# Second layer of a three-stage kernel: block products summed in PSUM, multiplications on VectorE, plain products for two weight sets, waves of 8, 8 and 2 token tiles

## The chip, the core and the metric

The kernel runs on one core of a Trainium2 chip. The metric is the device time of one execution in microseconds (us). The engines are TensorE (PE for its matmuls, PEld for its weight loads), VectorE (DVE), ScalarE (ACT), GpSimd (POOL) and SyncE (SP, which issues the DMAs). All matrix products accumulate in PSUM, which has 8 banks of 128 x 512 float32.

## What is computed

```python
scores = scale * np.matmul(q, k.transpose(0, 1, 3, 2)) + bias      # attention, 4 x 8 heads, 576 tokens, depth 64
x = softmax(scores) @ v                                            # as 2304 tokens x 512
h = x @ w_in;  x = (h - np.tanh(h)) @ w_out                        # first layer, 512 -> 2048 -> 512
g = x @ w_gate                                                     # second layer, 512 -> 1536
silu = g * (1.0 / (1.0 + np.exp(-g)))
val = x @ w_val
return (silu * val @ w_out).astype(np.float32)                     # 1536 -> 512
```

Everything is float32. The change concerns the last four lines, and the hand-over from the first layer to them.

## The kernel before

**Products in three passes.** Each operand is split into a high part (the value rounded to the format that PE multiplies) and a low part (the rest). `matmul3` (L716) forms a product from three matmuls: high x high, high x low, low x high. A split costs one copy on ACT and one subtraction on DVE or POOL; all subtractions go through the helper `subtract` (L62).

**Second layer in quads.** For a pair of 128 x 2 output features ("weight set", 12 of them, gate and value in turn) and 768 of the 2304 tokens (three groups p), the 2 x 2 block product is a quad n, 36 in all: n // 3 is the weight set, n % 3 the token group. A quad is formed by the Strassen-Winograd scheme: seven products P1 to P7 (`PRODUCTS`, L927) of 6 matmuls of 384 columns each, in place of eight. The price are sums and differences: of weights (`combine_w`), of activations (`combine_x`, operands T1 to T4, from the accumulators acc of the first layer), and of results (`add`, `copy_one`). Three PSUM banks serve a quad (`QUAD_BANKS`): bank 0 for P1 and P2, bank 1 for P6, P7 and P4, bank 2 for P5 and P3. P1 is copied to SBUF as s1 by ACT, and DVE adds s1 to what stands in bank 1 after P6, then after P7, then after P4, so each of these products waits for DVE to have read the one before it.

**Pointwise part.** For a gate quad ACT takes the sigmoid, then block 0 is multiplied on DVE (`times_one`) and the other three blocks at once on POOL (`times_rest`, L1173, 1152 columns). For a value quad the same multiplications take the stored gate result, and the product goes to DRAM (`store`).

**Order of work.** The program order of each engine is its order on the chip. `begin` (L1184) interleaves the first quad with the last two output products of the first layer (tiles y). `step(n)` (L1206) handles the first products of quad n and the last ones of quad n - 1. Weights are read as raw 64-bit values and decoded ahead (`decode_first`, `decode_second`) on ACT, DVE and POOL, at places in the steps that `plan_decode` fixes.

**Output product.** `finish` (L1282) goes through the tokens in three waves of six tiles of 128 tokens. For each of the 12 feature chunks of a wave it loads 768 tokens back (DMA), splits them (`stage`: copy on ACT, subtraction on DVE) and runs 6 x 3 matmuls of 512 columns (tiles o). Results leave through three row buffers (`rows`).

## Time and profile before

| | |
|---|---|
| median of 3 runs | 1176.49 us (1172.83 to 1177.21) |
| profiled execution, its own time | 1175.12 us |
| its span, first to last instruction | 1173.3 us |
| PE busy | 1114.2 us, 95%, 7736 matmuls |
| DVE busy | 913.2 us, 78% |
| ACT busy | 742.0 us, 63% |
| POOL busy | 602.4 us, 51% |

Attention takes the first 294 us, the first layer runs to about 711 us, the second layer begins at 698.8 us between the first layer's last products, and the output product begins at 1009.4 us. A busy PE is not PE at its peak: matmuls are pipelined, so start-to-start distances are read instead of durations. Times in the rows below are in us from the start of the span, but "mean ns" in ns. In a timeline row the columns are start, duration, engine, line, operation, output tile <- input tiles, shape, number of merged instructions, and in brackets the idle time of the engine before the row with what ended it.

### The profile page before, as it was taken

Reading aid. Unit: us, or ns where it says so; the run is one execution under the profiler, and the core shown is the slowest. Engines: PE = TensorE matmul, PEld = TensorE weight load, DVE = VectorE, ACT = ScalarE, POOL = GpSimd, SP = SyncE. Lnnn points to the kernel's source line nnn. Section 1 sums busy time; section 2 is a strip of 40 time slices with the busy share of each in tenths; the row PEclk is TensorE's granted clock in tenths of the full one; section 3 lists DMA queues with packets and bytes.
Section 4 is the critical chain, followed back from the end, with each engine's and each line's share of the span. In section 5 each row is a group of like instructions: output and inputs, shape, how many; then the busy total and the mean of one; then the engine's idle time right before and its main releaser. Section 6 shows DMA issues by size and latency. Waiting matters only on the chain.

```text
span 1173.3 us, 21360 instructions
## 1 busy us (share of the span) xinstructions
PE 1114.2 (95%) x7736; PEld 924.1 (79%) x7736; DVE 913.2 (78%) x1732; ACT 742.0 (63%) x1463; POOL 602.4 (51%) x553
## 2 busy tenths in 40 slices
PE   8999999999999999999999996789999999899998
PEld 4577777777688888888888775788999899778886
DVE  7878999999699899889888899777777876873222
ACT  7989999998688887778778774333334334252222
POOL 3367777776363544355254445665666566660000
PEclk9999999999999999999999998899999999999999
DMA  5863535351112012011101100132231421554342
GB/s 193 278 191 89 146 95 156 88 164 40 37 55 72 19 54 60 13 55 55 36 19 36 36 1 1 36 126 89 91 107 48 152 90 67 189 182 159 94 158 85
DMA packets 92745, 107.46 MB, mean 92 GB/s; under 512 B 45280, under 2 KB 70112, under 8 KB 92640
## 3 DMA queue, kind: packets, MB, share of 16 engines
q1 hardware_dynamic: 92640, 106.10, 28.7%
q8 instruction: 61, 1.00, 0.4%
q14 instruction: 44, 0.36, 0.1%
HBM read 75.41 MB, written 30.67 MB: 90 GB/s over the span
## 4 chain that ended last, share of the span: by engine, by line
PE 69%; DVE 15%; ACT 5%; POOL 5%; issue 4%; DMA 2%; SPq 0%; POOLq 0%; DVEq 0%; ACTq 0%
PE h L720 14%; PE y L720 14%; PE b L720 12%; PE o L720 10%; PE x L436 7%; PE s L315 6%; DVE w L62 2%; PE pTa L381 2%; DVE bits_gate L1044 1%; DVE bits_gate L1035 1%; DVE bits_out L1044 1%; DMA bias<-bev 1%; PE pTb L381 1%; POOL bits_out L1037 1%; DVE acc L879 1%
## 5 line engine op out<-in xcount | busy, mean ns | idle before, releaser
L720 PE MATMUL y<-gh,w 128*128 128x512 f32 (+1 forms) x748 | 197.8, 369 | 3.2 <-POOL gh L62 1.5
L720 PE MATMUL h<-xh,w 128*128 128x512 f32 (+1 forms) x640 | 191.1, 369 | 0.0
L720 PEld LDWEIGHTS y<-gh,w 128*128 128x128 f32 x748 | 133.8, 188 | 28.9 <-POOL gh L62 2.5
L359 POOL TENSOR_SCALAR p<-p,r 128x576 f32<-128x576 f32 x144 | 109.2, 769 | 50.3 <-PE s L315 14.3
L720 PEld LDWEIGHTS h<-xh,w 128*128 128x128 f32 x640 | 116.9, 189 | 20.7 <-issue 0.5
L720 PE MATMUL h<-xl,w 128*128 128x512 f32 (+1 forms) x320 | 117.9, 368 | 0.0
L341 ACT ACTIVATE p<-p,m 128x576 f32<-128x576 f32 x144 | 111.1, 775 | 1.2 <-DVE m L330 0.8
L330 DVE CUSTOM_DVE_ANT_0 p<-s,bt 128x576 f32<-128x576 f32 x144 | 103.7, 753 | 10.5 <-PE s L315 10.3
L720 PE MATMUL o<-w,xh 128*128 128x512 f32 x324 | 100.0, 390 | 0.0
L826 ACT ACTIVATE sq<-h 128x512 f32<-128x512 f32 (+1 forms) x80 | 44.3, 554 | 64.2 <-PE h L720 64.2
L720 PE MATMUL b<-xh,w 128*128 128x384 f32 x288 | 81.0, 338 | 1.1 <-ACT s L1145 1.1
L720 PE MATMUL y<-gl,w 128*128 128x512 f32 (+1 forms) x212 | 78.9, 372 | 2.3 <-POOL gl L62 2.3
L720 PE MATMUL b<-xh,acc2r 128*128 128x384 f32 x288 | 80.5, 337 | 0.0
L315 PEld LDWEIGHTS s<-k,q 64*128 64x128 f32 x768 | 57.5, 184 | 28.4 <-issue 17.6
L436 PE MATMUL x<-pt,vn 128*64 128x256 f32 (+1 forms) x512 | 79.1, 421 | 0.2 <-DVE xl L451 0.2
L837 DVE TENSOR_TENSOR t<-h,sq 128x512 f32<-128x512 f32 (+1 forms) x80 | 51.4, 643 | 32.6 <-ACT th L827 32.2
L62 POOL TENSOR_TENSOR gl<-g,gh 128x512 fp32r<-128x512 f32 (+1 forms) x27 | 33.2, 1229 | 84.6 <-issue 42.1
L1173 POOL TENSOR_TENSOR sq<-sq,g 128x1152 f32<-128x1152 f32 x18 | 50.4, 2800 | 45.9 <-ACT g L1168 45.9
L315 PE MATMUL s<-k,q 64*128 64x288 f32 x768 | 72.9, 310 | 0.1
L720 PEld LDWEIGHTS o<-w,xh 128*128 128x128 f32 x324 | 61.1, 189 | 12.4
L1173 POOL TENSOR_TENSOR sq<-v,sq 128x1152 f32<-128x1152 f32 x18 | 53.1, 2948 | 31.4 <-DVE v L1150 31.4
L720 PE MATMUL o<-w,xl 128*128 128x512 f32 x162 | 63.5, 392 | 5.3 <-DVE xl L62 5.3
(209 smaller groups left out, 3099.9 us busy)
## 6 DMA issues: line engine op xcount, KB each, us to landing
raw_out<-in_moe_w_out_dram SPq DMA_DIRECT2D x28, 512.0 KB, 3.5
s<-sq SPq DMA_DIRECT2D x36, 384.0 KB, 2.6
bias<-bev SPq DMA_DIRECT2D x36, 320.0 KB, 3.5
bt<-bias SPq DMA_DIRECT2D x16, 576.0 KB, 4.9
xh<-s SPq DMA_DIRECT2D x24, 384.0 KB, 3.6
raw_in<-in_moe_w_in_dram SPq DMA_DIRECT2D x16, 512.0 KB, 3.8
raw_gate<-in_moe_w_gate_dram SPq DMA_DIRECT2D x12, 512.0 KB, 5.0
raw_val<-in_moe_w_val_dram SPq DMA_DIRECT2D x12, 512.0 KB, 3.6
```

The lines of the kernel that those rows point to most:

```text
L62: (engine or nc.gpsimd).tensor_tensor(out, a, b, ALU.subtract)
L315: nc.tensor.matmul(self.st[u][j][:, e, 0:HALF], lhs, k[r, y, e * HALF:(e + 1) * HALF], start=n == 0, stop=n == 2,)
L330: nc.vector.tensor_tensor_reduce(out=p[:, n, :].rearrange("p (e f) -> p e f", e=2), in0=ps[n][:, :, 0:HALF], in1=bt[:, n, :].rearrange("p ...
L341: nc.scalar.activation(p[:, n, :], p[:, n, :], AF.Exp, bias=m[:, n:n + 1], scale=-1.0, accum_out=ls[:, n:n + 1],)
L359: nc.gpsimd.tensor_scalar(p[:, n, :], p[:, n, :], r[:, n:n + 1], 1.0, ALU.mult, ALU.mult)
L381: nc.tensor.transpose(half[h][:, 64 * m:64 * m + 64], p[r, j, k:k + 128], self.ident[r, r])
L436: nc.tensor.matmul(ps[r, 0:n], lhs, rhs, start=c == 0, stop=c == 4)
L720: nc.tensor.matmul(out, lhs[a], rhs[b], start=first and n == 0, stop=last and n == 2, skip_group_check=again)
L826: nc.scalar.activation(u, h, AF.Square)
L837: nc.vector.tensor_tensor(t, h, u, ALU.mult)
L1044: nc.vector.scalar_tensor_tensor(w, q["m"], MIN_HIGH * MIN_HIGH, w, ALU.is_ge, ALU.mult)
L1173: self.nc.gpsimd.tensor_tensor(to, self.rest(n), q["g"] if n // 3 % 2 == 0 else to, ALU.mult)
```

## The change

- **Sums in PSUM.** ACT copies P1 from bank 0 into bank 1 of the same quad (`copy_one`), and P6, P7 and P4 accumulate on that copy. ACT copies bank 1 to SBUF after P6 (u2) and P5 to SBUF (p5); DVE adds p5 to bank 1 after P7, and u2 to bank 2 after P3. P2 moves from step n to step n + 1.
- **Multiplications on DVE.** Blocks 0 and 2 are multiplied on DVE straight from PSUM (`point_one`), blocks 1 and 3 together from SBUF (`times_pair`, 768 columns). POOL keeps the sums of decoding and of `combine_w`.
- **Plain products.** The quads 0 to 5 (`PLAIN`, the first two weight sets) use no scheme: four blocks of 12 matmuls each, in four banks in turn, each multiplied from its bank as soon as it stands. Their weight sets need no sums, and the activations only the splits of the four blocks. The differences T1 to T4 are formed later (`later`, `flush_later`), between the blocks of the quads 0 to 5.
- **Waves.** The output product runs in waves of 8, 8 and 2 token tiles; a stage is 1024 tokens of one chunk, and in the last wave 256 tokens of four chunks. Three loads are in flight, nine row buffers stand ready, and the last tile leaves in two halves, copied by DVE and ACT. Stage 0 is loaded and split one step earlier.
- Buffers are moved to make room (`kept`, the accumulators in halves, other slots); decoding has other places in the steps.

```diff
+        self.kept = ctx.enter_context(self.tc.tile_pool(name="b_kept", bufs=1)).tile([128, 3, 512], F32, name="kept")
...
+PLAIN = 6
+SET_SLOTS = ((16, 17, 18, 19, 27, 28, 29), (20, 21, 22, 23, 24, 25, 26))
...
+PLAIN_BANKS = ("h2", "h0", "h1", "h3")
...
+BLOCKS = ((0, 0), (1, 0), (0, 1), (1, 1))
+WAVES = ((0, 8), (8, 8), (16, 2))
+LAST_C = 4
...
+        mixed = V if p == 2 else G
+        self.queue += [
+            high("B11", b11), high("B21", b21), low("B11", b11), low("B21", b21, mixed),
+            high("B12", b12), high("B22", b22), low("B12", b12), low("B22", b22, mixed),
+        ]
+        one = [high("T1", b11), low("T1", b11)]
+        three = [high("T3", b12, 2), low("T3", b12)]
+        self.later += [((1, 1, 2)[p], f) for f in (
+            sub(b11, b12, b11), sub(b12, b22, b12), sub(b22, b22, b11), high("T2", b22, 0), sub(b21, b21, b22),
+            low("T2", b22), high("T4", b21, 4), low("T4", b21), *(() if p else three),
         )]
-        self.queue += [(t2, f) for f in (high("T2", b22, 0), low(V, "T2", b22))]
-        self.queue += [(t3, f) for f in (high("T3", b12, 2), low(G, "T3", b12))]
-        self.queue += [(t4, f) for f in (high("T4", b21, 4), low(V, "T4", b21))]
-    def flush(self, n, now):
-        while n and (f := next((f for f in self.queue if f[0] <= now), None)):
-            self.queue.remove(f)
-            f[1]()
+        self.later += [(p + 4, f) for f in one]
+        if p:
+            self.later += [(p + 3, f) for f in three]
+        self.later.sort(key=lambda f: f[0])
...
+            if plain:
+                self.sets[s] = dict(
+                    A11=(h1[:, L], l1[:, L]), A12=(h1[:, R], l1[:, R]), A21=(h2[:, L], l2[:, L]), A22=(h2[:, R], l2[:, R]),
+                )
...
+            when = ((n - 6, 1), (n - 5, 0), (n - 5, 1), (n - 4, 0), (n - 3, 0), (n - 3, 1), (n - 3, 1), (n - 2, 0))
+            for at, f in sorted(zip(EARLY.get(s, when), work), key=lambda e: e[0]):
+                add(*at, *f)
...
+            add(n + 2, 0, self.split_out, c)
             add(n + 1, 1, self.decode_second, q)
-            add(n + 2, 2, self.split_out, c)
-            add(n, 2, self.decode_first, q)
+            add(n + 1, 0, self.decode_first, q)
...
-        first = k in ("P1", "P5", "P6")
+        first = k in ("P1", "P5")
...
     def copy_one(self, n):
+        banks = self.quads[n]["banks"]
+        if banks[1] is None:
+            banks[1] = self.bank(QUAD_BANKS[n % 2][1], f"b1_{n}")
+        self.nc.scalar.copy(banks[1][:, 0:U2], banks[0][:, 0:U2])
...
+    def copy_two(self, n):
         q = self.quads[n]
-        q["s1"] = self.shared.tile([128, U2], F32, tag=f"one{n % 2}", name=f"s1_{n}")
-        self.nc.scalar.copy(q["s1"], q["banks"][0][:, 0:U2])
-    def add(self, n, to, bank, b=None):
+        q["u2"] = self.shared.tile([128, U2], F32, tag=f"one{n % 2}", name=f"u2_{n}")
+        self.nc.scalar.copy(q["u2"], q["banks"][1][:, 0:U2])
...
+        out = self.sq[n % 3][:, 1 + 2 * i] if self.is_gate(n) else self.pair(n)[:, i]
+        self.nc.vector.tensor_tensor(out, q["banks"][bank][:, 0:U2], q[b], ALU.add)
+    def point_one(self, n, at, src):
+        to = self.sq[n % 3][:, at]
+        if self.is_gate(n):
+            g = self.pair(n)[:, 2]
+            self.nc.scalar.activation(g, src, AF.Sigmoid)
+            self.nc.vector.tensor_tensor(to, src, g, ALU.mult)
+        else:
+            self.nc.vector.tensor_tensor(to, src, to, ALU.mult)
+    def sigmoid_pair(self, n):
+        if self.is_gate(n):
+            self.nc.scalar.activation(self.pair(n)[:, 0:2], self.sq[n % 3][:, 1::2], AF.Sigmoid)
+    def times_pair(self, n):
+        to = self.sq[n % 3][:, 1::2]
+        self.nc.vector.tensor_tensor(to, to, self.pair(n)[:, 0:2], ALU.mult)
+        self.done(n)
...
-        self.nc.gpsimd.tensor_tensor(to, self.rest(n), q["g"] if n // 3 % 2 == 0 else to, ALU.mult)
...
+    def block(self, n, k):
+        nc = self.nc
+        i, j = BLOCKS[k]
+        self.quad(n)
+        bank = self.bank(PLAIN_BANKS[k], f"c{k}_{n}")[:, 0:U2]
+        for m in range(2):
+            A, X = self.sets[n // 3][f"A{i + 1}{m + 1}"], self.operands[n % 3][f"B{m + 1}{j + 1}"]
+            for dc in range(2):
+                matmul3(
+                    nc, bank, [t[:, 128 * dc:128 * dc + 128] for t in A], [t[:, dc] for t in X],
+                    m == dc == 0, m == dc == 1,
+                )
+        self.point_one(n, 2 * i + j, bank)
...
     def begin(self):
         m, n1 = self.moe, self.moe.n1
-        self.product(0, "P1")
-        self.copy_one(0)
+        self.block(0, 0)
+        self.flush(8)
         m.out_matmuls(n1 - 2)
-        self.flush(2, n1)
-        for k in ("P2", "P6"):
-            self.product(0, k)
-        self.add(0, 0, 1)
-        self.flush(2, n1)
-        self.product(0, "P5")
-        self.sigmoid_one(0)
-        self.flush(99, n1)
+        self.flush_later(3, 1)
+        self.block(0, 1)
         m.out_matmuls(n1 - 1)
-        self.product(0, "P7")
-        self.add(0, 2, 1)
-        self.add(0, 2, 2, 2)
         self.combine_x(2)
-        self.flush(4, n1)
-        self.decode(0, 2)
+        self.flush(2)
+        self.block(0, 2)
+        self.flush(4)
+        self.block(0, 3)
+        self.flush(2)
+        self.done(0)
+        for part in range(3):
+            self.decode(0, part)
+    def plain(self, n):
+        for k in range(4):
+            if (n, k) == (PLAIN - 1, 3):
+                self.product(PLAIN, "P1")
+                self.copy_one(PLAIN)
+            self.block(n, k)
+            self.flush(2)
+            self.flush_later(2, n)
+            if k < 3:
+                self.decode(n, k)
+        self.done(n)
     def step(self, n):
-        own = n < NQ
-        more = lambda k: self.flush(k, self.moe.n1)
-        if own:
+        own, before = n < NQ, n > PLAIN
+        if own and before:
             self.product(n, "P1")
-        if n > 1:
-            self.add(n - 1, 2, 1)
-            self.add(n - 1, 2, 2, 2)
-        if own:
+        if before:
+            self.add(n - 1, 1, 1, "p5")
+        if own and before:
             self.copy_one(n)
-        self.times_one(n - 1)
-        more(2)
+        if n - 2 in self.quads:
+            self.times_pair(n - 2)
+        self.flush_later(3, n)
+        if before:
+            self.product(n - 1, "P2")
+        self.decode(n, 0)
+        if before:
+            self.point_one(n - 1, 0, self.quads[n - 1]["banks"][0][:, 0:U2])
+            self.product(n - 1, "P4")
+            self.point_one(n - 1, 2, self.quads[n - 1]["banks"][1][:, 0:U2])
+        self.decode(n, 1)
         if own:
             self.product(n, "P6")
-            self.add(n, 0, 1)
-        more(3)
-        self.decode(n, 0)
-        self.product(n - 1, "P4")
-        self.add(n - 1, 1, 1)
-        more(3)
-        self.product(n - 1, "P3")
-        self.add(n - 1, 0, 2, 0)
-        more(99)
-        self.decode(n, 1)
-        self.sigmoid_rest(n - 1)
-        self.times_rest(n - 1)
-        self.store(n - 1)
+            self.copy_two(n)
+        if n == NQ - 1:
+            self.stage_split(0, 0, 768)
+        if before:
+            self.product(n - 1, "P3")
+            self.add(n - 1, 0, 2, "u2")
         if own:
-            self.decode(n, 2)
-            for k in ("P5", "P2", "P7"):
-                self.product(n, k)
-            self.sigmoid_one(n)
-        del self.quads[n - 1]
+            self.product(n, "P5")
+            self.copy_five(n)
+        if before:
+            self.sigmoid_pair(n - 1)
+        if own:
+            self.product(n, "P7")
+        else:
+            self.times_pair(n - 1)
...
+    def evict(self, at):
+        nc = self.nc
+        row, o = self.rows(at), self.o.pop(at)
+        to = self.out[128 * at:128 * at + 128, :]
+        if at < NT // 128 - 1:
+            (nc.vector.tensor_copy if at % 2 else nc.scalar.copy)(row, o)
+            nc.sync.dma_start(out=to, in_=row)
+        else:
+            for j, copy in enumerate((nc.vector.tensor_copy, nc.scalar.copy)):
+                half = slice(256 * j, 256 * j + 256)
+                copy(row[:, half], o[:, half])
+                nc.sync.dma_start(out=to[:, half], in_=row[:, half])
     def finish(self):
         self.o = {}
-        nt = 2 * U2 // 128
-        n = 3 * len(self.outs)
-        for f in range(n):
-            self.stage(f + 2, 0)
-            if f == 0:
-                self.out_tiles(0, range(0, 2))
-                self.step(NQ)
-            self.stage(f + 1, 1)
-            self.stage(f + 1, 2)
-            self.out_tiles(f, range(0 if f else 2, nt))
+        self.stages = [(w, (c,)) for w in range(2) for c in range(len(self.outs))]
+        self.stages += [(2, range(c, c + LAST_C)) for c in range(0, len(self.outs), LAST_C)]
+        self.stage_load(0, 0, 768)
+        self.step(NQ - 1)
+        self.stage_load(0, 768, 1024)
+        self.stage_load(1)
+        self.stage_load(2)
+        self.stage_split(0, 768, 1024)
+        self.stage_load(3)
+        self.out_tiles(0, range(2))
+        self.step(NQ)
```

Three places show how the order moves. The first is PE in the step of quad 14 (third token group, a gate quad): a name as b1_13 is bank 1 of quad 13. Before, the row of P1, P6 of quad 14, then P4 and P3 of quad 13:

```order
L720 MATMUL b0_14_11007<-xh_58,w5_5928 128x384
L720 MATMUL b0_14_11007<-xl_59,w5_5928 128x384
L720 MATMUL b0_14_11007<-xh_58,w5_5928 128x384 x2
L720 MATMUL b0_14_11007<-xl_59,w5_5928 128x384
L720 MATMUL b0_14_11007<-xh_58,w5_5928 128x384
L720 MATMUL b1_14_11019<-acc1r_10120,w5_5928 128x384 x6
L720 MATMUL b1_13_10943<-w5_5928 128x384 x6
L720 MATMUL b2_13_10986<-xh_58,w5_5928 128x384
```

The same place after:

```order
L720 MATMUL b0_14_10897<-xh_58,w5_5928 128x384
L720 MATMUL b0_14_10897<-xl_59,w5_5928 128x384
L720 MATMUL b0_14_10897<-xh_58,w5_5928 128x384 x2
L720 MATMUL b0_14_10897<-xl_59,w5_5928 128x384
L720 MATMUL b0_14_10897<-xh_58,w5_5928 128x384
L720 MATMUL b0_13_10822<-xh_58,w5_5928 128x384
L720 MATMUL b0_13_10822<-xl_59,w5_5928 128x384
L720 MATMUL b0_13_10822<-xh_58,w5_5928 128x384 x2
L720 MATMUL b0_13_10822<-xl_59,w5_5928 128x384
L720 MATMUL b0_13_10822<-xh_58,w5_5928 128x384
L720 MATMUL b1_13_10830<-w5_5928 128x384 x6
L720 MATMUL b1_14_10905<-acc11r_10159,acc21r_10250 128x384 x6
```

P2 of quad 13 (b0_13) now stands between P1 of quad 14 and P4 of quad 13, and P6 of quad 14 comes after P4.

The second place is DVE in the same step. The names s1, u2 and p5 are copies by ACT, v the pair buffer, sq the stored gate result, bits_gate and m_gate weights under decoding. Before:

```order
L1150 TENSOR_TENSOR sq_13_10950<-b1_13_10943,s1_13_10940 128x384
L1150 TENSOR_TENSOR sq_13_10950<-b2_13_10986,sq_13_10950 128x384
L1162 TENSOR_TENSOR sq_13_10950<-b0_13_10931,g1_13_11005 128x384
L1150 TENSOR_TENSOR sq_14_11026<-b1_14_11019,s1_14_11016 128x384
L1150 TENSOR_TENSOR sq_13_10950<-b1_13_10943,s1_13_10940 128x384
L1150 TENSOR_TENSOR sq_13_10950<-b2_13_10986,sq_13_10950 128x384
L1044 SCALAR_TENSOR_TENSOR bits_gate7_10980<-m_gate7_11042,bits_gate7_10980 128x512
```

After:

```order
L1199 TENSOR_TENSOR sq_14_10896<-b1_14_10905,p5_14_10952 128x384
L1217 TENSOR_TENSOR sq_13_10821<-sq_13_10821,v_13_10919 128x2x384
L62 TENSOR_TENSOR w5_5928<-bits_gate6_10785,w5_5928 128x512
L1207 TENSOR_TENSOR sq_14_10896<-b0_14_10897,v_14_10982 128x384
L1207 TENSOR_TENSOR sq_14_10896<-b1_14_10905,v_14_10982 128x384
L62 TENSOR_TENSOR w5_5928<-bits_gate7_10859,w5_5928 128x512
L1057 TENSOR_SCALAR bits_val6_10999<-raw_val6_10846 128x512
L1058 SCALAR_TENSOR_TENSOR bits_val6_10999<-raw_val6_10846,bits_val6_10999 128x512
L1199 TENSOR_TENSOR sq_14_10896<-b2_14_10945,u2_14_10936 128x384
```

Five sums and one multiplication a quad have become two sums (L1199), two multiplications from PSUM (L1207) and one from SBUF (L1217); the decoding stands between the multiplications and the last sum.

The third place is DVE at the end of the first layer, behind its last item (t_79, g_79). Before:

```order
L843 SCALAR_TENSOR_TENSOR g_79_9955<-s2_79_9947,t_79_9956 128x512
L845 COPY_PREDICATED g_79_9955<-sq_79_9944,h_79_9915 128x512
L62 TENSOR_TENSOR w0_967<-acc0_5932,w0_967 128x768
L62 TENSOR_TENSOR acc1_5933<-acc1_5933 128x2x384
L62 TENSOR_TENSOR xl_59<-acc1_5933,xh_58 128x2x384
L1150 TENSOR_TENSOR sq_0_10023<-b1_0_10016,s1_0_9994 128x384
```

After, where c0_0 and c1_0 are the first two blocks of quad 0:

```order
L848 COPY_PREDICATED g_79_9832<-kept_5955,h_79_9795 128x512
L62 TENSOR_TENSOR xl_59<-acc10_5934,xh_58 128x2x384
L1207 TENSOR_TENSOR kept_5955<-c0_0_9862,v_0_9875 128x384
L62 TENSOR_TENSOR acc00_5932<-acc00_5932 128x2x384
L62 TENSOR_TENSOR acc00_5932<-acc01_5933,acc00_5932 128x2x384
L62 TENSOR_TENSOR acc01_5933<-acc01_5933,acc00_5932 128x2x384
L1207 TENSOR_TENSOR kept_5955<-c1_0_9893,v_0_9875 128x384
```

The differences of the activations now stand behind the multiplication of the first block, between the multiplications of the plain quads.

## Rows read from the trace of the kernel before

**Rows 1.** Windows: busy time, instructions, granted clock (PEclk) in stretches of the second layer

```profile
core 0: us, PE busy (x) PEld busy (x) DVE busy (x) ACT busy (x) POOL busy (x), PEclk, DMA share, GB/s
718.00:725.00 7.00, 6.45 (x21) 6.06 (x22) 6.37 (x11) 4.19 (x6) 2.86 (x2) 0.55 0.01 4
...
732.00:742.00 10.00, 2.87 (x7) 1.97 (x8) 8.85 (x8) 4.72 (x9) 8.51 (x6) 0.50 0.00 0
...
752.00:762.00 10.00, 9.77 (x56) 9.78 (x57) 7.69 (x16) 3.05 (x5) 6.87 (x5) 1.00 0.17 54
...
1056.00:1173.30 117.30, 112.76 (x498) 93.02 (x496) 33.35 (x37) 27.50 (x36) 2.27 (x2) 0.99 0.39 124
...
794.09:841.33 47.24, 44.55 (x253) 43.60 (x253) 36.05 (x55) 16.62 (x28) 29.26 (x21) 1.00 0.28 95
```

**Rows 2.** Timeline of PE, two neighbouring products of a steady step

```profile
868.88 1.20 PE L720 MATMUL b<-acc1r,w 128*128 128x384 f32 x6
869.92 0.33 PE L720 MATMUL b<-xh,w 128*128 128x384 f32 x1
```

**Rows 3.** Timeline of PE: marks and waits of the second layer

```profile
698.77 0.33 PE L720 MATMUL b<-xh,w 128*128 128x384 f32 x1
...
718.55 2.26 PE L720 MATMUL b<-acc0r,w 128*128 128x384 f32 x6 [3.61 <-DVE acc L879]
...
741.78 2.29 PE L720 MATMUL b<-w 128*128 128x384 f32 x6 [6.01 <-DVE sq L1150]
...
752.23 1.33 PE L720 MATMUL b<-w 128*128 128x384 f32 x6 [1.46 <-DVE sq L1150]
...
1009.38 0.63 PE L720 MATMUL o<-w,xh 128*128 128x512 f32 x2
...
1013.03 0.50 PE L720 MATMUL o<-w,xl 128*128 128x512 f32 x1 [3.02 <-DVE xl L62]
...
1168.37 0.39 PE L720 MATMUL o<-w,xl 128*128 128x512 f32 x1
```

**Rows 4.** Waits of PE from 750 to 1005 us: total us, times, longest

```profile
PE b L720 <- DVE v L1150: 8.6, 6, 3.0
PE b L720 <- DVE sq L1150: 7.4, 5, 1.5
```

**Rows 5.** Timeline of all engines around one wait of PE

```profile
859.18 2.68 POOL L1173 TENSOR_TENSOR sq<-v,sq 128x1152 f32<-128x1152 f32 x1
859.22 3.19 DVE L62 TENSOR_TENSOR w<-bits_gate,w 128x512 fp32r<-128x512 f32 x1 [0.37 <-ACT w L1073]
...
862.46 0.48 ACT L1145 COPY s<-b 128x384 f32<-128x384 f32 x1 [1.96 <-PE b L720]
...
864.22 1.28 POOL L1037 TENSOR_TENSOR bits_val<-bits_val,r_val 128x512 int32<-128x512 int32 x1 [2.35 <-DVE bits_val L1036]
...
864.57 0.56 DVE L1150 TENSOR_TENSOR v<-b,v 128x384 f32<-128x384 f32 x1
```

**Rows 6.** Groups of POOL in six steps (794.09 to 841.33 us)

```profile
L1173 POOL TENSOR_TENSOR sq<-v,sq 128x1152 f32<-128x1152 f32 x3 | 8.8, 2931 | 4.9 <-DVE v L1150 4.9
L1173 POOL TENSOR_TENSOR sq<-sq,g 128x1152 f32<-128x1152 f32 x3 | 8.3, 2763 | 7.5 <-ACT g L1168 7.5
```

**Rows 7.** DVE: differences on acc as a group of the run, then four sums

```profile
L62 DVE TENSOR_TENSOR acc<-acc 128x768 f32<-128x768 f32 x12 | 18.1, 1510 | 0.8 <-POOL xl L62 0.6
...
717.72 2.47 DVE L879 TENSOR_TENSOR acc<-y,acc 128x512 f32<-128x512 f32 x4
```

**Rows 8.** Timeline of DVE in the output product

```profile
1041.11 1.78 DVE L1044 SCALAR_TENSOR_TENSOR bits_out<-m_out,bits_out 128x512 f32<-128x512 f32 x1 [1.18 <-POOL bits_out L1037]
...
1043.87 0.95 DVE L62 TENSOR_TENSOR xl<-xh 128x768 fp32r<-128x768 f32 x1
1046.00 1.77 DVE L1044 SCALAR_TENSOR_TENSOR bits_out<-m_out,bits_out 128x512 f32<-128x512 f32 x1 [1.18 <-POOL bits_out L1037]
```

**Rows 9.** Timeline of DVE, its last instruction

```profile
1169.64 0.69 DVE L1279 COPY rows<-o 128x512 f32<-128x512 f32 x1 [0.75 <-ACT rows L1279]
```

211 lines of the change are left out of this document (108 added, 103 removed), and 8 rows, old and new, of the table EARLY.

## The prediction

> **What bounds the kernel now.** I read the marks of PE first, since PE is the busiest engine and the chain of work that ended last runs mostly over it. The second layer begins on PE at 698.77, the output product at 1009.38, and the last matmul starts at 1168.37 [rows 3]. Then the price of a matmul without waiting. Six matmuls of 384 columns start within 869.92 - 868.88 = 1.04 us, so one costs 0.1733 us [rows 2]. From 1056 to the end of the last matmul (1168.37 + 0.23 = 1168.60) 498 matmuls of 512 columns take 112.6 us, 0.2266 us each [rows 1, 3].
>
> With these two prices each stretch splits into work and loss. The opening, up to the wait that ends at 752.23, holds 21 products (126 matmuls) of the second layer and the last 24 matmuls of the first: 21.8 + 5.4 = 27.3 us of work in 53.5 us, so 26.2 us are lost. The steps, 752.23 to 1009.38, hold 229 products (1374 matmuls): 238.1 us of work in 257.2, so 19.0 us are lost. The output product, 1009.38 to 1168.60, holds 648 matmuls of 512 and 12 of 384 columns: 148.9 us in 159.2, so 10.3 us are lost. From 1168.60 to the end of the span are 4.7 us. So 55.5 us before the tail are not work of PE, and everything that the change can win lies there.
>
> Next, who causes it. In the opening PE waits 3.61 us for sums on DVE and 6.01 us for DVE again, and behind such waits the granted clock is 0.55 and 0.50, its lower level of 1.2 GHz; from 752 on it is 1.00, 2.4 GHz, although a wait of 1.46 us lies in it [rows 1, 3]. In the steps all listed waits of PE are for DVE, 8.6 and 7.4 us, and six steps take 47.24 us where 252 matmuls are worth 43.7 [rows 1, 4]. One such wait shows its cause: a multiplication on POOL runs 2.68 us, and a subtraction on DVE that starts beside it, both inputs in SBUF, takes 3.19 us and ends just after it. A DVE sum with one input in PSUM takes 0.56 us beside another POOL instruction [rows 5]. So POOL's long multiplications, 17.1 of its 29.3 us in six steps [rows 1, 6], hold up DVE, and DVE holds up PE.
>
> **The extra products.** A plain quad has 48 matmuls for 42; six quads add 36 x 0.1733 = +6.2 us. They lie on PE's path and nothing hides them.
>
> **The opening.** The plain quads 0 to 2 need only the splits of their own blocks. The waits for T2 to T4 and for the sums between products go, and the first multiplications wait for nothing but a sigmoid. A bank comes back after three further blocks, 3 x 12 x 0.1733 = 6.2 us, so one late multiplication is covered. What is late next is DVE as a whole. Until quad 6 it has 24 multiplications from PSUM (0.56 each [rows 5]: 13.4), six splits of blocks and 24 differences and splits for T1 to T4 (30 x 0.95 [rows 8]: 28.5), the four last sums onto acc (2.5 [rows 7]) and the decoding of one and a half weight sets. A set costs at most what six steps leave beside 36 sums and multiplications, (36.05 - 36 x 0.56) / 2 = 7.9 us [rows 1], so 11.9. That is 56 us; PE's own work there is 24 blocks and the first layer's 24 matmuls, 49.9 + 5.4 = 55.4 us. The two are level, and DVE starts with its list later than PE. Working through the list, multiplication by multiplication, I find slack of 1 to 3 us where PE would come back for a bank. About nine instructions of POOL (1.28 or less each [rows 5]) can each delay DVE. I take a loss of 5 us in place of 26.2: **-21.2**. Bounds: nothing lost, and the price of 1.51 us that the differences on acc had beside POOL's long instructions [rows 7], 30 x 0.56 = 17 us more, so 0 to 22 us; I stay near the low end since the long instructions are gone. [...]
>
> The start itself moves little: DVE no longer has differences between the last items of the first layer. I take **-0.5** (bounds 0 and -2).
>
> **The steps.** POOL loses 17.1 us in six steps and keeps 12.2. DVE had 36 instructions of 0.56 in six steps; it gets 24 of these and six pair multiplications, 768 columns, both inputs in SBUF. The nearest row is the split of 768 columns, 0.95 us [rows 8]: 36 x 0.56 = 20.2 becomes 24 x 0.56 + 6 x 0.95 = 19.1 us. So even with every delay of before kept, DVE has 35 us of work for 43.7 us of PE. ACT copies three times a quad instead of once, 0.48 us each [rows 5], 12 copies more or 5.8 us on 16.6 of 47.24 [rows 1]: covered.
>
> Every product now waits for something that stands at least two products back, 2.08 us. P6 needs the copy of P1, with P2 and P4 between. P7 needs the copy u2, with P3 and P5 between. P4 needs the sum with p5, with P1 and P2 of other quads between. The last is the tightest, since the sum stands on DVE behind the decoding of the step: about 2.5 us of it after the second multiplication, in 4.2 us. It has the 2.08 us on top. So I take a loss of 2 us for 30 quads in place of 19.0: **-17.0**. Bounds: nothing, and the rate of before, 19.0 / 32.7 x 30 = 17.4 us. I am near nothing because the waits of before hang on the POOL rows that go.
>
> The pair multiplication is where a rule can be weighed. Rows 5 show that DVE was held up by POOL where both its inputs lay in SBUF. The Trainium skill (SBUF — State Buffer, section Who interferes with whom) says that such a DVE instruction and a GpSimd instruction that reads SBUF exclude each other, whichever starts first, and that one with at most one SBUF input outside the two-port modes is free. By that rule the pair multiplications would meet POOL in 12.2 of 43.7 us and be held for half an instruction, 0.6 us, so 0.2 us a step on average on an engine with slack, and the sum would be the same; a kernel with the pair read from PSUM would be freer still.
>
> **The output product.** Before, a stage of PE is 18 x 0.2266 = 4.08 us, while decoding of the output weights goes round DVE and POOL in 1046.00 - 1041.11 = 4.89 us [rows 8]; this sets the pace until 1056, and the first stage waits 3.02 us for its split [rows 3]. A stage of eight tiles is 24 x 0.2266 = 5.44 us. The loop gets a split of 1024 columns (1.27 us by 0.95 x 4/3), which adds at most 0.32: 5.2 us, under 5.44. The first split now lies in the step before; its cover is P3, P5 and P7 of quad 35. Loads are issued three stages ahead. Matmuls stay at 648. I take a loss of 1.5 in place of 10.3: **-8.8** (bounds 0 and 6).
>
> **The tail.** The last copy starts 1169.64 - 1168.60 = 1.04 us after PE and takes 0.69 [rows 3, 9]. With nine row buffers and halves I take 0.15 and 0.4 (0.41 by the line through 0.56 at 384 and 0.69 at 512 columns): **-1.1** (bounds 0 and -1.3).
>
> **The sum.** 1173.3 + 6.2 - 21.2 - 0.5 - 17.0 - 8.8 - 1.1 = 1130.9 us of span. The profiled execution took 1175.12 us, 1.8 more than its span, and the median of the runs is 1176.49, 1.4 more again: **1134 us**, 3.6% faster.
>
> **The rivals.**
> - *DVE paces the opening.* The list of 56 us is level with PE, and if POOL's sums and the sigmoids hold it up more than I found, PE follows DVE. For it: 36.05 of 47.24 us busy even in the steps. Against it: the long POOL instructions are gone. At 9 to 14 us lost the time is 1138 to 1143. Chance 17%.
> - *The waits of the steps move instead of going.* P4 still waits for a DVE sum that stands behind decoding, with the same 2.08 us of cover as before. For it: in the order before, the same kind of wait lay there. Against it: what made DVE late. At the rate of before 17.4 - 2 = 15.4 us come back: 1149. Chance 10%.
> - *The change does not reach its aim in the output product*: the decoding loop gets as long as the larger split and both POOL sums in a row, over 5.44 us; +5: 1139. Chance 5%, and its time lies inside the first.
> - *Slower: the clock falls in the opening.* The plain blocks pass through four banks with a short wait at each when DVE is late. At 1.2 GHz a matmul of 384 columns takes 0.35 us or more, as in the slow rows (2.26 us for six by duration, 1.20 at full clock [rows 2, 3]). Over 55.4 us of work that costs up to 55 us: 1134 + 50 = 1184. It decides against the change only from 42 us on, three quarters of the opening at the low level. Against it: the clock stood at 1.00 across a wait of 1.46 us [rows 1, 3], and no wait in my list reaches 3 us. Chance 2%. The Trainium skill (TensorE: Matmul & The Clock Gate, section A second HAM failure mode: psum-queue depth-cycling) reports such a kernel, which cycled through PSUM banks and swung between both levels; by it this rival would be likely, and the trace so far speaks against it.
>
> **How the numbers follow.** My own case, 1126 to 1138, has 66%. The range takes in the first two rivals and no-loss bounds: 1125 to 1150, with about 8% above (the clock, several losses at once) and 8% below. A difference of about 0.5%, 6 us, is what this measurement can tell from no change; 1170 and more has 5%, 2% of it beyond 1182.
>
> **What would show it.** In the trace after: the mark of the output product's first matmul 35 to 40 us earlier than 1009.38; six steps in 44 to 45 us; no wait over 2 us and a clock of 1.00 in every window of the opening; POOL multiplications absent, pair multiplications on DVE near 1 us; stages of eight tiles 5.4 to 5.5 us apart; the last copy within 0.3 us of the last matmul. Wrong would be: waits of PE for L1207 in the plain quads that add up to over 8 us, waits for the sum with p5 in most steps, or a clock near 0.5 between 700 and 755.

## The result and the profile after

The changed kernel takes 1128.04 us (median, 1127.42 to 1128.30) against 1174.76 us beside it: a ratio of 0.960 (95% interval 0.958 to 0.962), 4.0% faster. The forecast was 1134 in a range of 1125 to 1150. The profiled execution took 1127.98 us, its span is 1126.2.

The marks of PE, timeline of the changed kernel (start, us, engine, line, operation, output <- inputs, count, idle time before and what ended it):

```profile
696.76 0.33 PE L720 MATMUL c<-xh,w 128*128 128x384 f32 x1
...
751.27 0.41 PE L720 MATMUL b<-xh,w 128*128 128x384 f32 x1 [0.55 <-DVE sq L1209]
...
754.50 1.21 PE L720 MATMUL b<-w,acc21r 128*128 128x384 f32 x6
...
757.54 1.31 PE L720 MATMUL b<-w,acc21r 128*128 128x384 f32 x6 [0.70 <-ACT u L1188]
...
766.15 1.34 PE L720 MATMUL b<-acc00r,acc21r 128*128 128x384 f32 x6 [1.06 <-ACT u L1188]
...
799.79 1.20 PE L720 MATMUL b<-w,acc21r 128*128 128x384 f32 x6
...
843.68 1.20 PE L720 MATMUL b<-w,acc21r 128*128 128x384 f32 x6
...
972.00 0.63 PE L720 MATMUL o<-w,xh 128*128 128x512 f32 x2
...
1122.14 0.39 PE L720 MATMUL o<-w,xl 128*128 128x512 f32 x1
```

They answer to [rows 3]. With the two prices of the prediction (0.1733 and 0.2266 us a matmul) each stretch splits again into work and loss. The opening now holds the quads 0 to 5 and P1 of quad 6, and ends at 754.50: 57.74 us for 294 matmuls of 384 columns and 24 of 512, 56.39 us of work. The steps take 217.50 us for 1236 matmuls, 214.2. The output product, to 1122.14 + 0.23, takes 150.37 for 149.96.

| us | before | forecast | after |
|---|---|---|---|
| start of the second layer | 698.77 | -0.5 | 696.76 (-2.0) |
| extra products | | +6.2 | +6.2 |
| loss in the opening | 26.2 | 5 | 1.35 |
| loss in the steps | 19.0 | 2 | 3.3 |
| loss in the output product | 10.3 | 1.5 | 0.4 |
| last matmul to the end | 4.7 | 3.6 | 3.8 |

All waits of PE in the second layer up to the output product, and the three largest groups of waits of DVE in the steps, by the view of waits of the changed kernel (engine, tile, line <- who ended it: us in total, times, longest):

```profile
PE b L720 <- ACT u L1188: 1.8, 2, 1.1
PE b L720 <- DVE sq L1209: 0.5, 1, 0.5
```

```profile
DVE v L1199 <- PE b L720: 20.3, 15, 1.6
DVE w L62 <- ACT w L1085: 10.1, 9, 1.5
DVE sq L1199 <- PE b L720: 8.3, 7, 1.6
```

The relation has turned round. In [rows 4] PE waits for the sums v and sq of DVE; now these sums wait for PE. The busy times by windows of the changed kernel (PE, PEld, DVE, ACT, POOL, then granted clock, DMA share, GB/s):

```profile
712.00:742.00 30.00, 29.95 (x173) 29.63 (x172) 29.70 (x41) 13.67 (x24) 4.65 (x4) 1.00 0.16 49
...
799.00:843.00 44.00, 44.00 (x255) 43.77 (x254) 30.03 (x48) 22.16 (x44) 13.33 (x14) 1.00 0.31 102
```

In the opening, from 712 to 742 us, both PE and DVE are full and neither holds the other for long; the clock is at its upper level, 2.4 GHz, where [rows 1] had 0.55 and 0.50. In the steps DVE has 14 us to spare in 44, and POOL's share fell from 29.3 of 47.24 to 13.3 of 44.

### The profile page after: what moved, and what is told of

Its sections match the earlier page's. It is cut to its first block, busy times and chain, and to the rows that moved or that the text cites. A ratio compares the mean times of both kernels' runs of the same rounds, so it can differ in the third digit from the quotient of the medians.

```text
span 1126.2 us, 21423 instructions
## 1 busy us (share of the span) xinstructions
PE 1106.5 (98%) x7772; PEld 925.4 (82%) x7772; DVE 863.0 (77%) x1691; ACT 765.2 (68%) x1530; POOL 476.9 (42%) x499
## 4 chain that ended last, share of the span: by engine, by line
PE 84%; DVE 7%; ACT 3%; issue 1%; POOL 1%; DMA 1%; DVEq 0%; ACTq 0%; POOLq 0%
PE b L720 19%; PE h L720 17%; PE y L720 16%; PE o L720 13%; PE x L436 7%; PE s L315 6%; PE pTa L381 2%; DVE acc L62 1%; PE pTb L381 1%; ACT p L341 1%; DVE r L144 1%; PE pE L398 1%; DVE p L330 1%; DMA bias<-bev 1%; DVE w L62 1%
## 5 line engine op out<-in xcount | busy, mean ns | idle before, releaser
L359 POOL TENSOR_SCALAR p<-p,r 128x576 f32<-128x576 f32 x144 | 109.6, 773 | 49.9 <-PE s L315 15.7
L330 DVE CUSTOM_DVE_ANT_0 p<-s,bt 128x576 f32<-128x576 f32 x144 | 103.6, 753 | 10.3 <-PE s L315 10.3
L720 PE MATMUL o<-w,xh 128*128 128x512 f32 x324 | 102.7, 389 | 0.0
L720 PE MATMUL b<-xh,w 128*128 128x384 f32 x360 | 101.3, 335 | 0.5 <-DVE sq L1209 0.5
L720 PEld LDWEIGHTS h<-xl,w 128*128 128x128 f32 x320 | 60.4, 189 | 9.9
L720 PEld LDWEIGHTS b<-xh,w 128*128 128x128 f32 x360 | 65.9, 188 | 1.0 <-ACT acc21r L1102 0.8
L720 PE MATMUL b<-xl,w 128*128 128x384 f32 x180 | 60.2, 334 | 0.0
L829 ACT ACTIVATE sq<-h 128x512 f32<-128x512 f32 (+1 forms) x40 | 22.2, 556 | 50.7 <-PE h L720 50.7
L166 PE MATMUL bps<-r,cst 128*32 128x512 f32 x264 | 48.8, 634 | 7.6 <-DVE r L144 5.7
L720 PE MATMUL o<-w,xl 128*128 128x512 f32 x144 | 56.2, 390 | 0.0
```

Source lines behind the costliest of these rows:

```text
L166: nc.tensor.matmul(ps[0][32 * j:32 * j + 32].rearrange("p (t n) -> p n t", t=4), self.w2, R[j][:, 0:512].rearrange("p (n t) -> p n t", t=4 ...
L330: nc.vector.tensor_tensor_reduce(out=p[:, n, :].rearrange("p (e f) -> p e f", e=2), in0=ps[n][:, :, 0:HALF], in1=bt[:, n, :].rearrange("p ...
L359: nc.gpsimd.tensor_scalar(p[:, n, :], p[:, n, :], r[:, n:n + 1], 1.0, ALU.mult, ALU.mult)
L720: nc.tensor.matmul(out, lhs[a], rhs[b], start=first and n == 0, stop=last and n == 2, skip_group_check=again)
L829: nc.scalar.activation(u, h, AF.Square)
```

## The experiments

The theory behind the prediction was: POOL's long multiplications hold up DVE, DVE holds up PE, and the change wins because they are gone. The main rival: the new order wins, in which each product needs something that stands at least two products, or three plain blocks, back.

**Each half of it alone.** First the changed kernel with its pair multiplications on POOL again, then the kernel before with its multiplications on DVE, then that kernel without them.

```diff
 def times_pair          # e1, changed kernel
-        self.nc.vector.tensor_tensor(to, to, self.pair(n)[:, 0:2], ALU.mult)
+        self.nc.gpsimd.tensor_tensor(to, to, self.pair(n)[:, 0:2], ALU.mult)
 def times_rest          # e2, kernel before
-        self.nc.gpsimd.tensor_tensor(to, self.rest(n), ...)
+        self.nc.vector.tensor_tensor(to, self.rest(n), ...)
 def step                # e3, kernel before
-        self.times_rest(n - 1)
```

> The changed kernel with its 30 pair multiplications (768 columns, all inputs in SBUF) on POOL again. Theory A, that POOL's long multiplications hold up DVE and DVE holds up PE whatever the order of the products: by the row of 2.68 us for 1152 columns one takes 1.79 us, six steps hold 10.7 us of them where the kernel before had 17.1, so 0.63 of its loss of 3.5 us per six steps comes back, 2.2 us per six steps, 11 us in all: about 1139 us (1134 to 1142), with waits of PE for DVE. Theory B, that the new order of the products (each waits for something two products back, so that a late DVE is covered) is enough by itself: DVE instructions with both inputs in SBUF get longer beside POOL just the same, but PE waits less than 2 us more: 1128 to 1130 us.

> The kernel before with its 36 multiplications of 1152 columns on DVE instead of POOL, nothing else. DVE gets six of 1.42 us (0.95 us x 1152 / 768) in six steps on top of its 36.05 us, which still holds the time by which POOL stretched it. Theory A (POOL's multiplications stretch DVE, and that is what PE waits for): the 16 us of waits for v and sq in the steps go for the most part, about 1163 us (1158 to 1168). Theory B (the order of the products is what makes PE wait: a sum stands directly ahead of the product that needs its bank, and anything that lengthens DVE's list lengthens the wait): no gain, 1172 to 1185 us.

> The kernel before without its 36 multiplications of 1152 columns on POOL (left out: three quarters of the products of gate, sigmoid and value, so the output is another). Theory A: the loss of the steps falls from 19.0 to 3 to 5 us and some of the opening's goes too, 1155 to 1161 us; DVE's subtractions take 0.69 and 0.95 us where they took up to 3 us. Theory B: most of the waits for the sums v and sq stay, at least 10 us of them, 1166 us or more.

Measured: 1127.43 us (e1, 0.9605 of before, 0.9586 to 0.9623), 1152.76 (e2, 0.982), 1143.94 (e3, 0.975). The groups of DVE that subtract weight splits, from 780 to 980 us (columns: line, engine, operation, tiles, shapes, count | busy us, mean ns | idle time before and its cause): kernel before, e2, and e1.

```profile
L62 DVE TENSOR_TENSOR w<-bits_gate,w 128x512 fp32r<-128x512 f32 x12 | 18.7, 1562 | 1.5 <-ACT w L1073 1.5
```

```profile
L62 DVE TENSOR_TENSOR w<-bits_gate,w 128x512 fp32r<-128x512 f32 x12 | 8.2, 686 | 0.0
```

```profile
L62 DVE TENSOR_TENSOR acc21r<-bits_gate,acc21r 128x512 fp32r<-128x512 f32 x4 | 6.1, 1516 | 5.5 <-ACT acc21r L1102 5.5
```

In the kernel before the theory holds for the steps: with POOL's multiplications moved, the same subtraction falls from 1562 to 686 ns and the loss of the steps from 19.0 to 4.5 us (242.6 us from 750.86 to 993.44, 238.1 of work); without the multiplications it is 0.1. Both runs came out faster than theory A said. The gain of e2 is 21.5 us for the 11 expected, and 4.7 of it lies in the output product: its first wait is 0.86 us instead of the 3.02 of [rows 3], as the two decoding instructions ahead of the first split take 0.42 and 0.69 us instead of 2.90 and 1.63.

In the changed kernel POOL's multiplications cost PE next to nothing. In e1 POOL is busy for 24.8 of 44 us, its pair multiplications take 1.85 us each, and from the first block to the first tile o PE needs 275.9 us against 275.2. DVE is stretched again, but less: the group shown takes 1516 ns (692 in the changed kernel), the other three groups of the same subtraction 688, 989 and 1114 ns. Nor is e1 the full load of before: two of the three blocks are back on POOL, and DVE is busy for 26.8 of 44 us where [rows 1] has 36.05 of 47.24.

Theory B of e1 had the time nearly right, but not the reason. Every wait of PE in [rows 4] is one of P4, for the sum on P7. Two products stand between P7 and P4 before (P1 and P6) and after (P1 and P2), so in the steps this cover has not grown. What changed is what stands ahead of the sum in DVE's list. Before, it is decoding, stretched by POOL; behind the 3.19 us of [rows 5] follow, by the timelines of DVE and PE of the kernel before:

```profile
862.33 0.68 DVE L1044 SCALAR_TENSOR_TENSOR bits_val<-m_val,bits_val 128x512 f32<-128x512 f32 x1
...
863.99 0.55 DVE L1150 TENSOR_TENSOR v<-b,s 128x384 f32<-128x384 f32 x1
...
864.59 1.32 PE L720 MATMUL b<-w,acc2r 128*128 128x384 f32 x6 [1.13 <-DVE v L1150]
```

The sum on P7 starts up to 2.97 us after P7 has ended there. In e2 the decoding, no longer stretched, still stands ahead of it; the sum starts up to 1.65 us late (once 2.14), and two products cover nearly all of that. In the changed kernel the decoding stands ahead of the sum with u2, and the sum with p5 comes behind that one; for the quads 8 to 33 it starts 0.09 to 0.14 us after P7, once 0.45, and in e1 the same, with the stretched subtraction in the list (DVE's timeline of e1):

```profile
827.41 1.52 DVE L62 TENSOR_TENSOR acc21r<-bits_gate,acc21r 128x512 fp32r<-128x512 f32 x1 [1.38 <-ACT acc21r L1102]
...
832.30 0.56 DVE L1199 TENSOR_TENSOR v<-b,p 128x384 f32<-128x384 f32 x1 [0.30 <-PE b L720]
```

So either half takes most of the steps' loss away: in the old order moving the multiplications, in the new order what stands ahead of the sum. Which part of the new order does it (the place of the decoding, fewer sums on DVE, the copies on ACT) was not run by itself.

**How far this holds.** The run e1 with each pair multiplication done twice, and that run with the copy u2 ahead of the second decoding.

```diff
 def times_pair          # e8 and e10
+        for _ in range(2):
+            self.nc.gpsimd.tensor_tensor(to, to, self.pair(n)[:, 0:2], ALU.mult)
 def step                # e10 only
-        self.decode(n, 1)
         if own:
             self.product(n, "P6")
             self.copy_two(n)
+        self.decode(n, 1)
```

> The run with the pair multiplications on POOL, with each of them done twice (left as it comes out: the second factor is applied twice, so the output is another). POOL gets six more of 1.84 us in six steps, 24.7 + 11.0 = 35.7 of 44 us, more than the 29.3 of 47.24 in the kernel before. Theory B of the first run (the order of the products covers a late DVE): DVE is held longer than in the kernel before, and PE still loses no more than 4 us: 1127 to 1131. Theory A' (the order only helps while POOL's work is short; past the load of the kernel before the loss of the steps returns): 15 us or more come back, 1142 or more.

> The run with the pair multiplications done twice on POOL (1154.6 us, second factor applied twice, so the output is another), with P6 and the copy u2 ahead of the second part of the decoding. In that run all waits of the steps were for u2 on ACT, 18.4 us in 15 waits, and none for a sum on DVE. Theory A, that POOL reaches PE there through ACT's queue alone (the square of the weights waits on ACT for POOL, and u2 stands behind it): most of the 26.5 us go, 1128 to 1137 us. Theory B, that with so much work on POOL the decoding itself is too late and some other wait takes the place: 1146 us or more, with waits for the weights or for sums on DVE.

Measured: 1154.64 us (e8) and 1145.08 (e10). Theory A' of e8 held. The new order has a limit, between the 24.8 us of POOL in 44 of e1 and the 37.2 in 50.29 of e8; six steps of e8 take 50.29 us (817.65 to 867.94), of e10 46.45, of the changed kernel 43.9. Of the waits of PE in the steps of e8, 18.4 us are for u2 and 0.2 for a sum. One of them, followed back through the timelines of POOL, DVE, ACT and PE of e8:

```profile
810.98 4.09 POOL L1218 TENSOR_TENSOR sq<-sq,v 128x768 f32<-128x768 f32 x2
```

```profile
811.58 1.81 DVE L62 TENSOR_TENSOR acc20r<-bits_val,acc20r 128x512 fp32r<-128x512 f32 x1 [1.05 <-ACT acc20r L1102]
813.30 2.33 DVE L1066 SCALAR_TENSOR_TENSOR bits_gate<-m_gate,bits_gate 128x512 f32<-128x512 f32 x1
815.55 0.54 DVE L1207 TENSOR_TENSOR kept<-b,v 128x384 f32<-128x384 f32 x1
```

```profile
816.19 0.49 ACT L1206 ACTIVATE v<-b 128x384 f32<-128x384 f32 x1 [3.69 <-DVE kept L1207]
816.58 0.66 ACT L1055 ACTIVATE r_gate<-raw_gate 128x512 int32<-128x512 uint32 x1
817.12 0.48 ACT L1188 COPY u<-b 128x384 f32<-128x384 f32 x1
```

```profile
817.65 1.33 PE L720 MATMUL b<-acc00r,acc21r 128*128 128x384 f32 x6 [1.94 <-ACT u L1188]
```

POOL stretches two DVE instructions from 0.69 to 1.81 and 2.33 us. The multiplication behind them is late, the second sigmoid waits for it because both sigmoids of a quad use one buffer, and u2 stands behind that sigmoid in ACT's queue. Theory A of e10 (the square of the weights, waiting on ACT for POOL) was therefore the smaller part, and the time lies just under the 1146 us of theory B: moving the copy ahead takes back 9.6 of 26.6 us, and the waits become 5.1 us for the sum v on DVE and 3.7 for u2, which still stands behind the sigmoid.

**The remaining waits of the changed kernel.** The two waits for u2 are of the other kind, by ACT's timeline of the changed kernel:

```profile
765.08 0.66 ACT L1064 ACTIVATE m_gate<-raw_gate 128x512 f32<-128x512 f32 x1 [1.56 <-POOL acc20r L62]
765.64 0.46 ACT L1188 COPY u<-b 128x384 f32<-128x384 f32 x1
```

Run e6 moves the copy as e10 does, and gives the halves of the last tile two row buffers and two queues.

```diff
 def evict               # e6, besides the move in step
+                row = self.rows(at + 3 * j)
                 copy(row[:, half], o[:, half])
-                nc.sync.dma_start(out=to[:, half], in_=row[:, half])
+                (nc.sync, nc.scalar)[j].dma_start(out=to[:, half], in_=row[:, half])
```

> The changed kernel with two small moves. In each step the product P6 and the copy u2 on ACT come ahead of the second part of the decoding, and the two halves of the last tile go to two row buffers, the second one sent from ACT's queue. In the changed kernel PE waits twice for u2 in the first steps (0.70 and 1.06 us) while ACT stands at a square of the weights that waits for POOL. Theory A, that ACT's queue order alone makes these waits: they go, and with the halves side by side the tail gets 0.4 us shorter: 1.5 to 2.5 us less, 1125.5 to 1126.5. Theory B, that ACT is late for another reason or that DVE's or POOL's decoding, moved behind, takes the wait over: 1127.5 to 1129.5, with the wait under another line.

Measured: 1127.53 us (1125.89 to 1128.02), not to be told from 1128.04. From the first block to the first tile o it is 2.1 us shorter (273.1), but the decoding moved behind the copy is now late itself where the output product begins, by PE's timeline of e6:

```profile
971.53 1.32 PE L720 MATMUL b<-w 128*128 128x384 f32 x6 [0.84 <-DVE v L1199]
...
979.14 0.50 PE L720 MATMUL o<-w,xl 128*128 128x512 f32 x1 [0.65 <-DVE xl L62]
```

Theory B held: from the first block to the last matmul 425.1 us against 425.4. No run beat the changed kernel by more than can be told apart.

**The opening.** What it lost before was taken apart in the kernel before: without the 12 differences on acc (e4); also without the sums on the first two weight sets (e9); with its activation splits and its multiplications on DVE (e11); that without the differences (e12).

```diff
 def combine_x
-        sub = lambda eng, to, a, b: lambda: subtract(nc, to, a, b, eng)   # e4, e9, e12
+        sub = lambda eng, to, a, b: lambda: None
-            high("B11", b11), low(G, "B11", b11), ...                     # e11, e12
+            high("B11", b11), low(V, "B11", b11), ...
 def combine_w
-            subtract(nc, s3, w1[:, L], w2[:, L], G)                       # e9, and three more
+            if s > 1:
+                subtract(nc, s3, w1[:, L], w2[:, L], G)
```

> The kernel before without the 12 differences on acc from which T1 to T4 are made (left out: the subtractions alone, the splits of T1 to T4 stay, so the output is another). Theory C, that the opening of the kernel before was lost because its products need the whole chain of differences and splits from the first quad on: DVE's list gets 12 to 15 us shorter and PE's waits with it, and the clock stays up, so the opening's loss falls from 26.2 us to 8 or less: 1154 to 1158 us. Theory D, that it was lost to POOL's long instructions and to the multiplications by which banks come free: at least 18 of the 26.2 us stay, 1167 us or more.

> The kernel before without the 12 differences on acc and without POOL's four differences and sums on the weights of the first two sets (left out: these only, so the output is another; the products, the splits and the decoding stay). It takes away what plain products don't need, at the same 42 matmuls a quad. Without the differences on acc alone the gain was 10 us, and a wait of 8.6 us for a sum remained: that sum stood on DVE behind the split of a combined weight set, which waited for ACT and for POOL. Theory C2, that the opening was lost to both chains together: the long wait goes as well, with the slow matmuls behind it, and 16 to 20 of the opening's 26.2 us are saved: 1154 to 1158 us. Theory D2, that POOL's long multiplications and splits do it whatever the chains need: no more than another 3 us, 1161 us or more.

> The kernel before with the multiplications of 1152 columns and the 12 splits of 768 columns that lay on POOL in the opening on DVE, nothing left out. With the multiplications alone on DVE the time was 1152.8 us and the opening still lost 24.1 us (750.86 - 699.47 less 27.3 of work). DVE gets 12 x 0.95 = 11.4 us more in the opening, and the rows that POOL's splits stretched (differences of 1.55, splits of 2.0 and 2.4 us) go back to 0.95, about 10.7 us less: its list is as long as before. Theory E, that POOL's splits beside DVE's are what the opening lost to: PE waits shorter, the opening's loss falls to 14 us or less, 1143 us or less. Theory F, that the products of the first three quads stand too close behind the differences and splits in DVE's order, wherever these run: the loss stays at 20 us or more, 1149 us or more.

> The run before this one, with the 12 differences on acc left out (so the output is another). They take DVE 12 x 0.95 = 11.4 us. Alone, in the kernel before, leaving them out took 8.9 us off the opening's loss of 26.2 and left a wait of 8.6 us behind POOL's splits. Theory E and F together, that the opening lost to both, the differences in DVE's order and POOL's splits beside it: with both gone at most 8 us are lost, 16 us less than the 24.1, 1137 us or less. Theory G, that something else in it remains (the sums from PSUM behind which the first products stand): 12 us or more are lost, 1141 us or more.

| us | median | loss in the opening | in the steps |
|---|---|---|---|
| before | 1174.8 | 26.2 | 19.0 |
| e2, multiplications on DVE | 1152.8 | 24.1 | 4.5 |
| e3, no multiplications on POOL | 1143.9 | 23.7 | 0.1 |
| e11, and the activation splits | 1152.0 | 23.9 | 4.3 |
| e4, no differences | 1164.3 | 17.3 | 19.0 |
| e9, and no sums on two sets | 1166.5 | 17.4 | 21.8 |
| e12, as e11 without differences | 1144.8 | 17.4 | 3.9 |

(Losses by the same marks: in e12 742.65 - 697.94 less 27.3 of work.) Here POOL's multiplications are not the cause: without them (e3) 23.7 of 26.2 us stay. With the activation splits on DVE too it is 23.9, though DVE then has more to do itself. The differences are worth 6.5 to 8.9. About 17.4 us stay in all three runs without them. So theories C, C2 and E fell, F and G held, D2 held in time (1166.5) and D nearly (1164.3), but the cause that both name, POOL's long instructions, is not borne out by e3 and e11. What stays in e12 is seven waits of PE, 11.6 us in all, and slower matmuls (granted clock 0.66 from 726 to 733 us and 0.72 from 733 to 743). The longest wait, by PE's timeline of e12 and, behind it, DVE's:

```profile
732.49 2.29 PE L720 MATMUL b<-w 128*128 128x384 f32 x6 [5.63 <-DVE sq L1150]
```

```profile
729.13 1.70 DVE L1173 TENSOR_TENSOR sq<-sq,g 128x1152 f32<-128x1152 f32 x1 [0.38 <-ACT g L1168]
730.76 1.20 DVE L62 TENSOR_TENSOR acc2r<-bits_val,acc2r 128x512 fp32r<-128x512 f32 x1
731.89 0.54 DVE L1150 TENSOR_TENSOR sq<-b,s 128x384 f32<-128x384 f32 x1
```

The sum on P7 stands behind a multiplication and a weight split of the list, and P4, which needs its bank, comes only two products (2.08 us) after P7. DVE is late because its list is nearly full (busy for 12.9 of 14 us from 719 to 733), and the cover is too short. The six matmuls after the wait take 2.29 us for 1.20.

The plain products have a longer cover, three blocks, and one place in the changed kernel shows what it is worth. PE is done with the 14th block at 731.48 us, the multiplication of this block ends 6.4 us later, and PE takes the bank again at 737.94; the two matmuls there take 0.84 us instead of 0.51 (timelines of DVE and PE):

```profile
737.34 0.55 DVE L1209 TENSOR_TENSOR kept<-c,kept 128x384 f32<-128x384 f32 x1
...
737.55 0.84 PE L720 MATMUL c<-xh,w 128*128 128x384 f32 x2
```

That the plain products win by this distance alone, with the list of DVE as long as before, was not run by itself; that there is no other reserve in DVE is shown by the run that fills its list:

```diff
 def combine_x           # e5, changed kernel: the splits of T1 to T4 twice
-            subtract(nc, ops[name][1], src, ...)
+            for _ in range(2 if name[0] == "T" else 1):
+                subtract(nc, ops[name][1], src, ...)
```

> The changed kernel with the 12 splits of T1 to T4 on DVE done twice (same values again), 12 x 0.95 = 11.4 us more for DVE between 710 and 756, while everything else stays. In the trace of the changed kernel DVE has no idle time between 712 and 742 and PE none either; the multiplications of blocks 12 to 15 end within about 0.5 us of the moment at which PE wants their bank again. Theory A, that DVE stands exactly at the point where it begins to pace the opening: the five splits that lie ahead of block 14 move its multiplication 4.8 us later, PE waits about as long, and some of the later splits add to it: 1133 to 1138 us, with waits of PE for the multiplications in the plain quads. Theory B, that the three blocks between two uses of a bank (6.2 us) still cover it: at most 2 us, 1128 to 1130.

Measured: 1139.19 us, 11.2 more for 11.4 us of DVE; the loss of the opening grows by 8.5 us, that of the steps by 2.4. Windows of e5 and its waits of PE to 762:

```profile
712.00:742.00 30.00, 26.40 (x147) 24.98 (x146) 29.69 (x39) 10.80 (x19) 4.64 (x4) 1.00 0.11 36
```

```profile
PE c L720 <- DVE sq L1214: 2.3, 2, 1.3
PE c L720 <- DVE kept L1214: 2.1, 2, 1.5
PE c L720 <- DVE sq L1212: 1.5, 1, 1.5
```

Theory A, and a little more than its 1133 to 1138 us: DVE stands at the point where it begins to pace the opening. The clock stayed at 1.00 through waits of up to 1.5 us here.

**The waves.** The changed kernel with three waves of six.

```diff
-WAVES = ((0, 8), (8, 8), (16, 2))
+WAVES = ((0, 6), (6, 6), (12, 6))     # stages of 768 tokens, 36 in place of 27
```

> The changed kernel with the output product in three waves of six token tiles as before, 36 stages of 4.08 us of PE, the rest as changed. Theory A, that the waves of eight are what keeps PE ahead of the decoding loop (4.89 us a round in the kernel before): nine rounds of decoding lie in the output product, 9 x 0.8 = 7 us less the one or two stages that the weights are ahead: 1131 to 1136 us, with waits of PE for a split of s or of the weights. Theory B, that in the kernel before the loop only began late, behind POOL's last multiplications, and that six tiles would now do as well: 1127 to 1130.

Measured: 1132.89 us, 4.9 more. PE's timeline of e7 shows the decoding loop as the pace, 5.19 us a round for a stage of 4.08:

```profile
1000.09 0.50 PE L720 MATMUL o<-acc20r,xl 128*128 128x512 f32 x1 [0.81 <-DVE xl L62]
1005.29 0.50 PE L720 MATMUL o<-acc20r,xl 128*128 128x512 f32 x1 [0.82 <-DVE xl L62]
1010.48 0.50 PE L720 MATMUL o<-w,xl 128*128 128x512 f32 x1 [0.82 <-DVE xl L62]
```

Theory A. In the changed kernel the same loop goes round in 5.46 us, by its DVE timeline, where DVE waits only for POOL and not for PE:

```profile
1003.20 0.69 DVE L1066 SCALAR_TENSOR_TENSOR bits_out<-m_out,bits_out 128x512 f32<-128x512 f32 x1 [1.47 <-POOL bits_out L1059]
1003.81 1.22 DVE L62 TENSOR_TENSOR xl<-xh 128x1024 fp32r<-128x1024 f32 x1
...
1008.66 0.69 DVE L1066 SCALAR_TENSOR_TENSOR bits_out<-m_out,bits_out 128x512 f32<-128x512 f32 x1 [1.47 <-POOL bits_out L1059]
```

The longer split lies in the loop (1.22 us for 0.95, and 5.46 a round for 5.19). So a stage of eight tiles, 5.44 us, does not leave the loop behind; it is level with it, and since this split ends 3 us before its stage begins (1008.12), the difference of 0.02 us a round is not felt.

## Why the prediction was right, point by point

**The views and the places** were right: nearly all that was won lay in the three losses, and the sum missed the span by 4.7 us (1130.9 for 1126.2).

**Extra products:** 36 matmuls more in the page (7772 for 7736), on PE's path, as said.

**The opening (-21.2, came to -24.9)** is the term that was mis-sized. The list of DVE was taken as 56 us; the windows hold 51.7 us of DVE from 696.8 to 754.5. The decoding in it is 8.6 us instead of 11.9, which was worked out from steps in which POOL stretched it, and the splits run 0.95 and 1.19 us each. "The two are level" was right, as e5 shows, but a loss of 5 us was put where level with three blocks of cover meant 1.35. The reason given for the low end (the long POOL instructions are gone) carries little: in the kernel before they cost the opening 2.5 us (e3).

**The steps (-17.0, came to -15.7).** The price was about right, the place of the rest was not. P4 with its sum was named as tightest, since the sum was put behind the decoding of the step; it starts 0.1 us after P7 instead (and of the two products between, P2 is of the same quad, not of another). ACT was called covered because of its busy share, 22 of 44 us. The two waits are P7's for u2, on ACT, which stood in its queue at a decoding instruction. A busy share doesn't show what an engine's next instruction waits for. And the credit went to POOL alone, where e1 shows that the new order loses only 3.9 us with two of the three blocks back on it.

**The output product (-8.8, came to -9.9):** near in size, with some luck. The loop was put at 5.2 us with the longer split, 0.24 under a stage; it runs at 5.46, and at 5.19 already with the short split of e7, where 4.89 was carried over from before. The room that the argument counted on was not there, and the third rival's condition (over 5.44 us) was met without its price. Nearly half of the old loss had another cause, instructions of DVE stretched by POOL's last multiplications (10.3 to 5.6 in e2).

**Start, tail and median.** The start of the second layer scatters: 695.1 to 699.5 in the profiles of the seven kernels with the old beginning, 694.9 to 697.7 in the seven with the new, so -0.5 and -2.0 can't be told apart. The line through the two copies gives 0.43 us for a half, not 0.41 (measured 0.42 and 0.37). The tail gained 0.9 for 1.1, since the halves of the last tile run one after the other:

```profile
1122.56 0.42 DVE L1383 COPY rows<-o 128x256 f32<-128x256 f32 x1 [8.79 <-PE o L720]
...
1123.06 0.37 ACT L1383 COPY rows<-o 128x256 f32<-128x256 f32 x1 [2.63 <-DVE rows L1383]
```

The 1.4 us added for the median did not come (1127.98 and 1128.04).

**The rivals.** DVE as the pace of the opening shows as 0.5 us of waits, and comes in full with e5. Moved waits came as 1.8 us, on ACT instead of the sum; in e8 they are 18.4 us. The clock never fell: 1.00 in every window of the opening, although 24 plain blocks go through four banks in turn. The Trainium skill's report of a swing between both levels in such a cycle (TensorE: Matmul & The Clock Gate, section A second HAM failure mode: psum-queue depth-cycling) does not describe this kernel.

**The weighed rule.** Pair multiplications take 0.95 us; three of the 30 take 1.24 to 1.26 and one 1.88, on average 0.06 us more; 0.2 was forecast. The subtraction rows of the kernel before, e2 and e1 (1562, 686 and 1516 ns) agree with what the Trainium skill (SBUF — State Buffer, section Who interferes with whom) says of DVE instructions with two inputs in SBUF beside GpSimd.
